# Attention and FFN on one core: sums of W_out kept in SBUF, W_in read back from DRAM for each batch, k and v loaded in two halves, sums formed on VectorE

## The chip, the cores and the metric

One core of one Trainium2 chip runs one program. The metric is the device time of one execution in microseconds (us), lower is better; several executions are timed and their median is compared. The engines are PE (TensorE, with PEld for its weight loads), DVE (VectorE), ACT (ScalarE), POOL (GpSimd) and SP (SyncE, which issues nearly all DMAs of this kernel). A profile is one further execution, recorded by the hardware.

## The reference

```python
a = softmax(phi, over the 32 memory slots)                 # 8 batches, 8 heads, 576 rows
k_m = einsum('bhsm,bhsd->bhmd', a, k); v_m = einsum('bhsm,bhsd->bhmd', a, v)
attn = softmax(q @ k_m.T / 8)                              # 576 x 32 per head
x = (attn @ v_m) as rows of 512                            # 4608 x 512
h = x @ w_in;  g = h * sigmoid(h);  out = g @ w_out        # 512 -> 2048 -> 512
```

All is float32. The sums `k_m` and `v_m` are first divided by their softmax sums.

## The kernel before, in words

**Numbers in two parts.** A float32 operand is cut into a high and a low part in a format that TensorE multiplies in one pass (F32R). A product is high x high, high x low and low x high. W_out lies in SBUF as `wo_hi` and `wo_lo`, 16 chunks of 128 rows by 512 columns.

**P.** `attn @ v_m @ w_in` is done as `attn @ P` with P = `v_m @ w_in`, which has 256 rows (8 heads x 32) and 2048 columns. `p_mm` (L609) makes a quarter of P (512 columns) from `win` into the PSUM tile `bg`; `p_split` (L626) writes the high part on ACT (L629) and the low part on DVE (L631). W_in lies in the SBUF tile `win` all the time. P's homes are `pparts` (two quarters) and, from batch 2 on, two tiles `pm` for the other two.

**Batches 0 and 1** run 16 steps, one per chunk of 128 hidden columns: `ffn1` (h), `silu`, `split`, then `main_step` against the chunk of W_out into four PSUM banks. Batch 0 also converts the weights. The rows beyond 512 of two batches are handled together after each odd batch (`left_split`, `left_step`, later `left_st`).

**Batches 2 to 7** use the seven products of Strassen and Winograd instead of eight, on blocks of two row tiles by two chunks by two halves of columns. A batch has two halves `t` of eight steps `j`; one step is, in PE's order, `ffn1s` (12 matmuls into the PSUM tile `h`, L783), then what the table of events puts in that step, then `st_step` of the step before (21 matmuls, L814, into four banks `sum`). `forms` makes the seven left operands from silu: ACT writes `gbuf` (L794) and the first three high parts (L798), DVE the sums in `gbuf` (L799, L802, L803), the other four high parts (L804) and all the low parts `gparts` (L805). The silu of the next step writes the same `gbuf`, so it waits for L805. After the eighth step `st_out` combines the four banks: ACT copies two (L846), DVE does seven operations of 128x256 (L851), and SP stores the result (L862).

The seven right operands are four plain blocks of W_out (one of them replaced by the sum T1, `t1_load`) and three more sums of blocks. The sums are made once, in batch 1, by `w_forms`: POOL adds (L747 to L752), ACT and DVE cut the result into high and low parts in a tile `ring` (L755, L756), and a DMA writes it to DRAM (`saved`). From batch 2 on, each step reads three of them back into the four places of `ring`: `ring_load` asks for the next one after each use, 288 loads of 256 KB in all. In `st_step` the held blocks come first (8 matmuls with high left parts, 4 with low ones), then the three from the ring with 3 matmuls each. The four banks are filled in the order 0, 1, 2, 3.

**The order of the work.** PE's and (from batch 1) ACT's instructions stand as the code records them; DVE's and SP's are ordered by the scheduler. The attention for batch n = b + 1 is spread over the steps of batch b by a table of slots, `at_slot` (L921 to L925): `mx, sub, ex, em, tr, s0, s1, sx, se, ss, sn, sk` are the steps of the phi maximum, its fold and subtraction, its exp, `e_mm` (k_m and v_m from phi and the four k/v chunks), the transposes, the scores, their maximum, exp, sum, norm, and the way back. `p_mm` for the next batch is at steps 10, 12 and 14, its last quarter at step 0 of that batch. `load_kv` fetches the four k/v chunks (516 KB each) and a rest of the next batch right behind `e_mm`. The scores `s_all` use spare columns of the PSUM tile `h`, so the next `ffn1s` waits until DVE has turned them (L376, L378).

Of the kernel before, what the change touches and what calls it, by code (L numbers as in the profile page):

```python
# [19 lines left out]
P = 128  # L20
# [28 lines left out]
def attn_ffn_kernel(  # L49
# [19 lines left out]
    win = const.tile([P, NFC, NR, P], F32, name="win")  # L69
# [6 lines left out]
    pparts = const.tile([P, 2, 2, 2 * JW], F32R, name="pparts")  # L76
# [44 lines left out]
    raws, cvas, last_silu, last_split = {}, {}, [], []  # L121

    def w_load(w, part=None, few=False):
# [3 lines left out]
        if w not in raws:  # L127
            if w in HOMES:
                home = win[:, HOMES[w] : HOMES[w] + 4].rearrange("p k r f -> p (k r f)")
                raws[w] = home.bitcast(I64).rearrange("p (k f) -> p k f", k=2)  # L130
            else:
                raws[w] = sb.tile([P, 2, DMODEL], I64, tag="raw", name="raw", bufs=RAWB)
# [15 lines left out]
    def w_conv(w, part=None, steps="pcsahl"):  # L148
# [7 lines left out]
        if kind == "i":  # L156
            to = win[:, fc].rearrange("p k r f -> p k (r f)")
# [65 lines left out]
    def load_kv(b):  # L223
        queue = nc.scalar if b == 0 else None
        ts = []
        for c in range(FULLC):
            t = sb.tile([P, 2, NR, KVW], F32, tag="kv", name=f"kv{b}_{c}", bufs=FULLC)
            load(t.rearrange("p g r f -> p (g r f)"), kv[b, :, c * KVC : (c + 1) * KVC], queue=queue)
            ts.append(t)
        t = sb.tile([P, NR, KVW], F32, tag="kr", name=f"kr{b}", bufs=1)  # L230
        load(t.rearrange("p r f -> p (r f)"), kv[b, :, FULLC * KVC :], queue=queue)
        at[b]["kv"], at[b]["kr"] = ts, t
# [83 lines left out]
    def e_mm(b):  # L316
        e, er, kvt, kr = (at[b][k] for k in ("e", "er", "kv", "kr"))
        pt = beside_h(KVW) if b == 2 else banks(b)
        turns = [(c, p) for c in range(FULLC) for p in range(2)]
        if b == 0:  # L320
            turns.sort(key=lambda t: t[1])
        for c, p in turns:
            for r in range(NR):
# [5 lines left out]
                )  # L329
        for r in range(NR):  # L330
# [161 lines left out]
    def f_copy(u):  # L492
        if u == 0:
            first["left"] = sb.tile([P, P], F32, tag="mx", name="sleft", bufs=1)
        t = first["main", u] = sb.tile([P, 2, 2 * P], F32, tag="kv", name=f"sT{u}", bufs=FULLC)
# [98 lines left out]
    pj, more = {}, []  # L594

    def p_home(b, j):
        if b > 1 and j < 2:
            if not more:
                more.extend(sb.tile([P, 2, 2 * JW], F32R, tag="raw", name=f"pm{k}", bufs=RAWB) for k in range(2))
            home = [more[k][:, j] for k in range(2)]  # L600
        else:
            home = [pparts[:, k, j % 2] for k in range(2)]
        pj[b, j] = [x.rearrange("p (g f) -> p g f", g=2) for x in home]

    def p_mm(b, f, w, low=True):
        j = f // JW
        if f % JW == 0:
            p_home(b, j)
        hi, lo = pj[b, j]  # L609
        c = slice(f % JW, f % JW + w)  # L610
        bg = bgtile()
        kvT = at[b]["kvT"]
        for r in range(NR):
            for p in range(2):
# [3 lines left out]
                    win[D * p : D * (p + 1), f // P : (f + w) // P, r],  # L618
                    start=True, stop=True, skip_group_check=True,
                )  # L620
        if low:
# [73 lines left out]
    def store(key, rows, last=False):  # L695
        if key[0] == 0:
            o = sb.tile([P, DMODEL], F32, tag="raw", name="o", bufs=RAWB)
# [30 lines left out]
    saved = [hbm.tile([P, 4, DMODEL], F32, name=f"forms{j}") for j in range(NP)]  # L728
    ring = []
# [8 lines left out]

    def w_forms(j, step):


        if not ring:
            ring.append(sb.tile([P, 4, DMODEL], F32R, tag="raw", name="ring", bufs=RAWB))
        if step == 0:
            f = at[0]["forms", j] = sb.tile([P, 2, DMODEL], F32, tag="cva", name="wf", bufs=1)
            c = slice(2 * j, 2 * j + 2)
            nc.gpsimd.tensor_tensor(f, as_f32(wo_hi[:, c]), as_f32(wo_lo[:, c]), op=ALU.add)  # L747
            b11, b12, b21, b22 = (f[:, k, q * Q : (q + 1) * Q] for k in range(2) for q in range(2))
            nc.gpsimd.tensor_tensor(b11, b12, b11, op=ALU.subtract)
            nc.gpsimd.tensor_tensor(b12, b22, b12, op=ALU.add)  # L750
            nc.gpsimd.tensor_tensor(b22, b22, b11, op=ALU.add)
            nc.gpsimd.tensor_tensor(b21, b22, b21, op=ALU.subtract)  # L752
# [3 lines left out]
        nc.vector.tensor_tensor(ring[0][:, :, Q:], f, ring[0][:, :, :Q], op=ALU.subtract)  # L756
# [447 lines left out]
```

## Time and profile before

| | |
|---|---|
| median of 3 runs | 743.29 us (742.35 to 745.4) |
| the profiled execution | 746.09 us, of which the span from first to last instruction is 744.3 us |
| PE, PEld busy | 695.1, 602.6 us |
| DVE, ACT, POOL busy | 547.5, 305.8, 50.6 us |
| DMA | 146.36 MB, mean 197 GB/s |
| ring loads | 288 of 256 KB, 3.9 us from issue to landing in the median |

The profiled execution is 2.8 us above the median, 0.4%. Batch 0 ends near 106 us, batch 1 with its left rows near 212 us, batch 2 near 294.6, batch 3 near 391.6, batch 4 near 473.6, batch 5 near 572.5, batch 6 near 651.4 us.

How to read it: an engine's busy time is an average over stages. A row of the waits says which engine and line waited for whom, the sum in us, how often, and the longest. A row of the chain of waits is a piece of the sequence that ended last. A row of the groups has the operation with its tiles, out before in, its shape, the count, busy us and mean ns of one, and the idle time in front of it. "PEld" rows are weight loads, one ahead of each matmul.

### The profile page before, as it was taken

Reading aid. Unit: us, or ns where it says so; the run is one execution under the profiler, and the core shown is the slowest. Engines: PE = TensorE matmul, PEld = TensorE weight load, DVE = VectorE, ACT = ScalarE, POOL = GpSimd, SP = SyncE. Lnnn points to the kernel's source line nnn. Section 1 sums busy time; section 2 is a strip of 40 time slices with the busy share of each in tenths; the row PEclk is TensorE's granted clock in tenths of the full one; section 3 lists DMA queues with packets and bytes.
Section 4 is the critical chain, followed back from the end, with each engine's and each line's share of the span. In section 5 each row is a group of like instructions: output and inputs, shape, how many; then the busy total and the mean of one; then the engine's idle time right before and its main releaser. Section 6 shows DMA issues by size and latency. Waiting matters only on the chain.

```text
span 744.3 us, 15025 instructions
## 1 busy us (share of the span) xinstructions
PE 695.1 (93%) x5932; PEld 602.6 (81%) x5932; DVE 547.5 (74%) x1056; ACT 305.8 (41%) x565; POOL 50.6 (7%) x46
## 2 busy tenths in 40 slices
PE   8999989889899899888999899899899999999996
PEld 3577768777788788887899888788788989889896
DVE  4997897567876689748887579966678669766663
ACT  4877854423525243433424334442431525332320
POOL 0000030667300000000000000000000000000000
PEclk9999999999999999999999999999999999999999
DMA  9996721634566876587653876579564555566661
GB/s 343 309 329 202 290 90 72 230 126 177 209 188 190 294 210 186 159 263 249 191 171 99 259 242 201 148 198 311 163 188 131 144 157 179 164 192 178 194 187 54
DMA packets 70390, 146.36 MB, mean 197 GB/s; under 512 B 7088, under 2 KB 17456, under 8 KB 69296
## 3 DMA queue, kind: packets, MB, share of 16 engines
q1 hardware_dynamic: 69376, 142.63, 60.7%
q10 hardware_dynamic: 944, 2.77, 0.9%
q8 instruction: 47, 0.77, 0.4%
q14 instruction: 23, 0.19, 0.1%
HBM read 127.55 MB, written 17.83 MB: 195 GB/s over the span
## 4 chain that ended last, share of the span: by engine, by line
PE 47%; DMA 17%; DVE 14%; POOL 3%; ACT 3%; issue 3%; SPq 0%; DVEq 0%; ACTq 0%
PE sum L814 20%; DMA ring<-forms 17%; PE h L783 12%; PE lsum L814 5%; PE acc L691 3%; PE bg L615 2%; PE h L650 2%; DVE gparts L805 2%; PE accleft L691 1%; POOL wf L747 1%; DVE oo L851 1%; PE bg L324 1%; DVE pm L631 1%; DVE ring L756 1%; ACT gbuf L794 1%
## 5 line engine op out<-in xcount | busy, mean ns | idle before, releaser
L794 ACT ACTIVATE gbuf<-h 128x512 f32<-128x512 f32 x96 | 57.5, 599 | 297.5 <-PE h L783 209.1
L814 PE MATMUL sum<-ring,aparts 128*128 128x256 f32 x576 | 116.3, 293 | 22.2 <-DMA ring<-forms 18.2
L814 PEld LDWEIGHTS sum<-ring,aparts 128*128 128x128 f32 x576 | 88.1, 190 | 35.0 <-DMA ring<-forms 28.6
L805 DVE TENSOR_TENSOR gparts<-gbuf,aparts 128x896 fp32r<-128x896 f32 x96 | 104.5, 1088 | 9.0
L799 DVE TENSOR_TENSOR gbuf<-gbuf 128x256 f32<-128x256 f32 x96 | 40.8, 425 | 87.1 <-ACT gbuf L794 86.9
L814 PE MATMUL sum<-wo_hi,aparts 128*128 128x256 f32 x384 | 98.8, 290 | 0.0
L814 PE MATMUL sum<-wo_lo,aparts 128*128 128x256 f32 x384 | 95.5, 282 | 0.0
L783 PE MATMUL h<-aparts,pm 128*128 128x288 f32 x576 | 85.6, 298 | 5.4 <-DVE sc L378 5.4
L691 PE MATMUL acc<-wo_hi,gparts 128*128 128x512 f32 x256 | 87.6, 402 | 2.4 <-DVE gparts L667 2.2
L814 PEld LDWEIGHTS sum<-wo_hi,aparts 128*128 128x128 f32 x384 | 72.5, 189 | 17.4 <-issue 11.1
L783 PEld LDWEIGHTS h<-aparts,pm 128*128 128x128 f32 x576 | 79.6, 191 | 6.4 <-issue 6.3
L783 PE MATMUL h<-aparts,pparts 128*128 128x288 f32 x576 | 83.8, 294 | 0.0
L814 PE MATMUL sum<-ring,gparts 128*128 128x256 f32 x288 | 80.6, 280 | 0.0
L783 PEld LDWEIGHTS h<-aparts,pparts 128*128 128x128 f32 x576 | 78.1, 188 | 0.0
L814 PEld LDWEIGHTS sum<-wo_lo,aparts 128*128 128x128 f32 x384 | 72.7, 189 | 0.0
L814 PE MATMUL sum<-wo_hi,gparts 128*128 128x256 f32 x384 | 63.0, 286 | 1.3 <-DVE gparts L805 0.8
L650 PEld LDWEIGHTS h<-aparts,pparts 128*128 128x128 f32 x372 | 52.7, 192 | 13.0 <-issue 2.9
L650 PE MATMUL h<-aparts,pparts 128*128 128x288 f32 x372 | 57.4, 304 | 6.0 <-ACT gleft L677 2.2
L691 PEld LDWEIGHTS acc<-wo_hi,gparts 128*128 128x128 f32 x256 | 48.5, 191 | 17.2 <-DVE gparts L667 4.9
L814 PEld LDWEIGHTS sum<-wo_hi,gparts 128*128 128x128 f32 x384 | 52.6, 191 | 3.5 <-DVE gparts L805 3.1
L814 PEld LDWEIGHTS sum<-ring,gparts 128*128 128x128 f32 x288 | 54.2, 188 | 0.0
L691 PE MATMUL acc<-wo_lo,gparts 128*128 128x512 f32 x128 | 51.1, 399 | 1.0 <-DVE wo_lo L178 0.9
(199 smaller groups left out, 1055.3 us busy)
## 6 DMA issues: line engine op xcount, KB each, us to landing
ring<-forms SPq DMA_DIRECT2D x288, 256.0 KB, 3.9
kv<-in_kv SPq DMA_DIRECT2D x28, 516.0 KB, 6.9
q<-in_q SPq DMA_DIRECT2D x16, 576.0 KB, 6.2
forms<-ring SPq DMA_DIRECT2D x8, 1024.0 KB, 4.1
raw<-in_w_in SPq DMA_DIRECT2D x14, 512.0 KB, 6.3
out<-oo SPq DMA_DIRECT2D x27, 256.0 KB, 2.4
raw<-in_w_out SPq DMA_DIRECT2D x6, 1024.0 KB, 5.0
phi<-in_phi SPq DMA_DIRECT2D x7, 576.0 KB, 4.9
```

The source lines that it names most:

```text
L324: nc.tensor.matmul(pt[p][M * r : M * (r + 1), :KVW], e[:, p, c, M * r : M * (r + 1)], kvt[c][:, p, r], start=c == 0, stop=False, skip_grou ...
L615: nc.tensor.matmul(bg[M * r : M * (r + 1), p, :w].rearrange("p (k f) -> p k f", f=P), kvT[D * p : D * (p + 1), 1, r], win[D * p : D * (p + ...
L631: nc.vector.tensor_tensor(lo[:, :, c], bg[:, :, :w], hi[:, :, c], op=ALU.subtract)
L650: nc.tensor.matmul(h[:, hf, :HALF], wt[:, p, fs], a[:, p, hf * HALF : (hf + 1) * HALF], start=n[hf] == 0, stop=n[hf] == 5, skip_group_chec ...
L691: nc.tensor.matmul(acc[key], gt[:, cs], wt[:, fc], start=fc == 0 and n == 0, stop=fc == NFC - 1 and n == 2)
L747: nc.gpsimd.tensor_tensor(f, as_f32(wo_hi[:, c]), as_f32(wo_lo[:, c]), op=ALU.add)
L756: nc.vector.tensor_tensor(ring[0][:, :, Q:], f, ring[0][:, :, :Q], op=ALU.subtract)
L783: nc.tensor.matmul(h[:, i, :HALF], wt[:, p, f : f + P], a[:, p], start=n == 0, stop=n == 5)
L794: nc.scalar.activation(gbuf[:, :MAIN].rearrange("p (i f) -> p i f", i=2), h[:, :, :w], AF.Silu)
L799: nc.vector.tensor_tensor(g[:, 4:6], g[:, :1].broadcast_to([P, 2, P]), g[:, 1:3], op=ALU.subtract)
L805: nc.vector.tensor_tensor(lo, g[:, 1:], hi, op=ALU.subtract)
L814: nc.tensor.matmul(sums[bank][:, place * Q : (place + 1) * Q], gt[:, k], wt, start=bank not in begun, stop=True, skip_group_check=True,)
```

## The change

- The three sums per step stay in SBUF as `kept`, 24 tiles of 128x512 float32 (high and low halves side by side); `ring`, `ring_load` and the 288 loads are gone. Only T1 still goes through DRAM.
- The room comes from W_in and from two k/v chunks. W_in is in four tiles `w0` to `w3`; in batch 0 `win_save` writes them to DRAM, and in batch 1 `kept` takes their places. From batch 2 on, `win_load` brings a quarter of W_in (1 MB) into the very place `h0` to `h3` in which that quarter of P will lie, `p_mm` reads it from there, and then the parts of P overwrite it. A quarter can come when the last `ffn1s` of the batch that reads the old P is done.
- From batch 3 on `load_kv` and `e_mm` go in two halves: chunks 0 and 1 are used at step 5, chunks 2 and 3 come into the same two places and are used at step 7.
- `w_forms` adds on DVE instead of POOL.
- `st_step` does all seven high parts first, then all seven low ones, and fills the banks in the order 0, 3, 1, 2.
- The slots move: the tables below the code show it.

```diff
     def w_forms(j, step):
...
         if step == 0:
+            while len(kept) < 3 * j + 3:
+                keep(*homes_left.pop(0))
             f = at[0]["forms", j] = sb.tile([P, 2, DMODEL], F32, tag="cva", name="wf", bufs=1)
             c = slice(2 * j, 2 * j + 2)
-            nc.gpsimd.tensor_tensor(f, as_f32(wo_hi[:, c]), as_f32(wo_lo[:, c]), op=ALU.add)
+            nc.vector.tensor_tensor(f, as_f32(wo_hi[:, c]), as_f32(wo_lo[:, c]), op=ALU.add)
...
-        nc.scalar.activation(ring[0][:, :, :Q], f, AF.Copy)
-        nc.vector.tensor_tensor(ring[0][:, :, Q:], f, ring[0][:, :, :Q], op=ALU.subtract)
-        load(saved[j], as_f32(ring[0]))
...
+        for t, i, e in runs:
+            src, to = f[:, n : n + e - i], t[:, i:e]
+            nc.scalar.activation(to[:, :, :Q], src, AF.Copy)
+            nc.vector.tensor_tensor(to[:, :, Q:], src, to[:, :, :Q], op=ALU.subtract)
+            n += e - i
+        load(saved[j], as_f32(t1[:, 0]))
...
-        held = ((0, 0, 0, b11), (0, 1, 2, b21), (1, 0, 6, b22), (1, 1, 4, b12))
+        t3, t4, t2 = ((x[:, :Q], x[:, Q:]) for x in kept[3 * j : 3 * j + 3])
+        todo = (
+            (0, 0, 0, b11), (0, 1, 2, b21), (3, 0, 1, t4), (1, 0, 6, b22), (1, 1, 4, b12), (2, 0, 5, t2), (2, 1, 3, t3)
+        )
         for terms in (HIGH, LOW):
-            for bank, place, k, w in held:
+            for bank, place, k, w in todo:
                 product(bank, place, part, k, w, terms)
-        for bank, place, k in ((2, 0, 5), (2, 1, 3), (3, 0, 1)):
-            r = ring[0][:, next(used) % 4]
-            product(bank, place, part, k, (r[:, :Q], r[:, Q:]), HIGH + LOW)
-            ring_load()
...
+    win_saved = [hbm.tile([P, 4, NR, P], F32, name=f"win_saved{k}") for k in range(4)]
+
+    def win_save():
+        for k in range(4):
+            load(win_saved[k], win[k])
+
+    def win_load(b, k):
+        t = wins[b, k] = sb.tile([P, 4, NR, P], F32, tag=f"h{k}", name=f"win{b}_{k}", bufs=1)
+        load(t, win_saved[k])
...
-                ev(b, 1.5 * j + 3, w_forms, j, 1)
+                ev(b, 1.5 * j + 2.5, w_forms, j, 1)
         else:
-            ev(b, 0, p_mm, b, (3 if b > 2 else 2) * JW, JW)
-            if b == 2:
-                ev(b, 2, p_mm, b, 3 * JW, JW)
-            else:
+            ev(b, 0, win_load, b, 3)
+            ev(b, 1, p_mm, b, 2 * JW, JW)
+            ev(b, 3, p_mm, b, 3 * JW, JW)
+            if b > 2:
...
-            else (0, 1, 3, 5, 6, 7, 7, 9, 10, 11, 11, 13)
+            else (1, 2, 4, 5, 8, 9, 9, 10, 11, 12, 13, 14)
...
+            ev(b, em, e_mm, n, range(2))
+            ev(b, em, load_kv, n, range(2, FULLC))
+            ev(b, em + 2, e_mm, n, range(2, FULLC))
+            if n + 1 < B:
+                ev(b, em + 2, load_kv, n + 1, range(2))
...
-            for j in range(3):
-                ev(b, 10 + 2 * j, p_mm, n, j * JW, JW)
+            for k in range(3):
+                ev(b, 6 + k if b == 1 and k < 2 else 10 + 2 * k, win_load, n, k)
+            for k in range(2):
+                ev(b, (12 if b == 1 else 13) + 2 * k, p_mm, n, k * JW, JW)
```

DVE's order in the middle of batch 2, around the turning of the scores into `sc`, before (steps 7 and 8; `x<-sum` is the first operation of `st_out`):

```order
L376 STREAM_TRANSPOSE sc_2434<-bg 128x512
L805 TENSOR_TENSOR gparts<-gbuf,aparts 128x896
L376 STREAM_TRANSPOSE sc_2434<-bg 128x512
L378 STREAM_TRANSPOSE sc_2434<-h 128x64 x2
L413 TENSOR_REDUCE smx<-sc_2434 128x36
L417 TENSOR_TENSOR sc_2434<-sc_2434,smx 128x1152
L799 TENSOR_TENSOR gbuf<-gbuf 128x256
L802 TENSOR_TENSOR gbuf<-gbuf 128x128
L803 TENSOR_TENSOR gbuf<-gbuf 128x128
L804 CAST aparts<-gbuf 128x512
L851 TENSOR_TENSOR x<-sum_2083,oo 128x256
L805 TENSOR_TENSOR gparts<-gbuf,aparts 128x896
```

The same place after (steps 8 and 9; lines have moved by some twenty, so L874 is `st_out`, L823 to L829 is `forms`, L387 and L389 turn the scores):

```order
L874 TENSOR_TENSOR oo<-oo 128x256
L874 TENSOR_TENSOR oo<-x,oo 128x256
L874 TENSOR_TENSOR oo<-x,sum_2121 128x256
L823 TENSOR_TENSOR gbuf<-gbuf 128x256
L826 TENSOR_TENSOR gbuf<-gbuf 128x128
L387 STREAM_TRANSPOSE sc_2573<-bg 128x512
L827 TENSOR_TENSOR gbuf<-gbuf 128x128
L387 STREAM_TRANSPOSE sc_2573<-bg 128x512
L828 CAST aparts<-gbuf 128x512
L389 STREAM_TRANSPOSE sc_2573<-h 128x64
L829 TENSOR_TENSOR gparts<-gbuf,aparts 128x896
L389 STREAM_TRANSPOSE sc_2573<-h 128x64
```

The turning of the scores stood a step ahead of `st_out`; now all seven operations of `st_out` are ahead of it, and the last turn out of `h` stands behind the low parts.

DVE's order where batch 2 ends and batch 3 begins, before (`pparts<-bg` is the low part of the last quarter of P, `aparts<-aT` the low part of the attention's second half):

```order
L631 TENSOR_TENSOR pparts<-bg,pparts 128x1024
L851 TENSOR_TENSOR x<-sum_2574,oo 128x256
L851 TENSOR_TENSOR x<-sum_2574,x 128x256
L851 TENSOR_TENSOR oo<-oo 128x256
L851 TENSOR_TENSOR oo<-x,oo 128x256
L851 TENSOR_TENSOR oo<-oo 128x256
L851 TENSOR_TENSOR oo<-x,oo 128x256
L851 TENSOR_TENSOR oo<-x,sum_2575 128x256
L799 TENSOR_TENSOR gbuf<-gbuf 128x256
L802 TENSOR_TENSOR gbuf<-gbuf 128x128
L452 TENSOR_TENSOR aparts<-aT_2784,aparts 128x2x288
L803 TENSOR_TENSOR gbuf<-gbuf 128x128
```

And after (`mt` is the start of the next phi maximum, `pm` the low part of the third quarter of P):

```order
L823 TENSOR_TENSOR gbuf<-gbuf 128x256
L874 TENSOR_TENSOR oo<-oo 128x256
L874 TENSOR_TENSOR oo<-x,oo 128x256
L874 TENSOR_TENSOR oo<-x,sum_2608 128x256
L826 TENSOR_TENSOR gbuf<-gbuf 128x128
L256 TENSOR_TENSOR mt<-phi_2849 128x512
L827 TENSOR_TENSOR gbuf<-gbuf 128x128
L646 TENSOR_TENSOR pm<-bg,pm 128x1024
L828 CAST aparts<-gbuf 128x512
L463 TENSOR_TENSOR aparts<-aT_2844,aparts 128x2x288
L829 TENSOR_TENSOR gparts<-gbuf,aparts 128x896
L257 TENSOR_TENSOR mx<-mt 128x256
```

The low part of P moved from ahead of `st_out` to behind it, into the middle of `forms` of step 0, and the phi maximum joined it there.

DVE's order early in batch 1, before (L665 and L667 are the split of the ordinary step; `wf` is the sum of blocks that POOL has formed, five rows per group on POOL):

```order
L667 TENSOR_TENSOR gparts<-gbuf,gparts 128x512
L756 TENSOR_TENSOR ring<-wf,ring 128x4x256
L665 CAST gparts<-gbuf 128x512
L667 TENSOR_TENSOR gparts<-gbuf,gparts 128x512
L756 TENSOR_TENSOR ring<-wf,ring 128x4x256
```

And after (L680 and L682 are the split; `t` and `kept` are the low parts of the sums):

```order
L769 TENSOR_TENSOR wf<-wo_hi,wo_lo 128x1024
L771 TENSOR_TENSOR wf<-wf 128x256
L772 TENSOR_TENSOR wf<-wf 128x256
L680 CAST gparts<-gbuf 128x512
L773 TENSOR_TENSOR wf<-wf 128x256
L682 TENSOR_TENSOR gparts<-gbuf,gparts 128x512
L774 TENSOR_TENSOR wf<-wf 128x256
L680 CAST gparts<-gbuf 128x512
L789 TENSOR_TENSOR t_1370<-wf,t_1370 128x256
L682 TENSOR_TENSOR gparts<-gbuf,gparts 128x512
L789 TENSOR_TENSOR kept<-wf,kept 128x256
L789 TENSOR_TENSOR kept<-wf,kept 128x2x256
```

Five additions and two or three subtractions per group now stand between the casts of the ordinary steps.

More of the change, by code (lines that the diff above doesn't have):

```diff
@@ L727, in attn_ffn_kernel @@
     TF = 7 * P
[L728 to L729 removed]
+    saved = [hbm.tile([P, DMODEL], F32, name=f"forms{j}") for j in range(NP)]
+    kept, kept_at = [], []
+    homes_left = [("r2", 4), ("w0", 4), ("w1", 4), ("kv2", 2), ("kv3", 2), ("w2", 4), ("w3", 4)]
     form_src = gbuf.rearrange("p (n f) -> p n f", f=P)
```

111 lines of the change are left out of this document (58 added, 53 removed).

## The prediction

> **What bounds the kernel now.** I read the page first, then the busy time by batch, then the waits, then the chain of waits. The page says how full the engines are and what the end hung on:
>
> ```profile
> PE 695.1 (93%) x5932; PEld 602.6 (81%) x5932; DVE 547.5 (74%) x1056; ACT 305.8 (41%) x565; POOL 50.6 (7%) x46
> ...
> PE 47%; DMA 17%; DVE 14%; POOL 3%; ACT 3%; issue 3%; SPq 0%; DVEq 0%; ACTq 0%
> ```
>
> TensorE is full most of the time, yet 17% of the chain runs through DMA and 14% through DVE. By stretches (time, then busy us of PE, PEld, DVE, ACT and POOL, granted clock, DMA share, GB/s): batch 1 without its left rows, batch 3, batch 6 and batch 7.
>
> ```profile
> 106.00:200.00 94.00, 84.87 (x599) 68.15 (x600) 66.70 (x92) 37.34 (x61) 44.08 (x36) 0.96 0.40 151
> 294.60:391.60 97.00, 89.64 (x818) 81.31 (x817) 74.01 (x156) 34.44 (x68) 0.00 (x0) 1.00 0.68 206
> 572.50:651.40 78.90, 76.69 (x728) 69.94 (x727) 60.19 (x118) 32.82 (x65) 0.00 (x0) 1.00 0.52 152
> 651.40:744.30 92.90, 84.76 (x663) 80.49 (x661) 54.21 (x114) 23.70 (x57) 0.00 (x0) 0.99 0.55 161
> ```
>
> Batch 1 wastes 9.1 us of PE, batch 3 7.4 us, batch 6, in which no k and v are loaded any more beside the ring, only 2.2 us. Who PE waited for (sum in us, times, longest):
>
> ```profile
> PEld sum L814 <- DMA ring<-forms: 28.6, 51, 2.4
> ...
> PEld sum L814 <- DVE oo L851: 4.0, 8, 1.2
> ...
> PE h L783 <- DVE sc L378: 5.4, 5, 1.1
> ...
> PEld sum L814 <- DVE gparts L805: 3.1, 9, 0.7
> ```
>
> ```profile
> ACT gbuf L794 <- DVE gparts L805: 77.9, 23, 5.3
> ```
>
> The ring is the largest wait, 51 times. The last row is the second bound: the silu of a step waits for DVE's low parts of the step before, since both use `gbuf`. What a step costs with no wait, from the chain (start, us, what):
>
> ```profile
> 410.93 1.58 PE h L783 x12
> 412.51 2.48 PE sum L814 x21
> ```
>
> So 4.06 us a step: 0.118 us a product.
>
> **The change, part by part.**
>
> *The ring goes.* A weight load takes 190 ns (the group row below) but one starts every 118, so each idle row is short by 0.07 us: 28.6 + 51 x 0.07 = 32.2 us. I take this; 28.6 is the low end, and 46.8 the high one, if PE's own 18.2 us never overlapped with them.
>
> ```profile
> L814 PE MATMUL sum<-ring,aparts 128*128 128x256 f32 x576 | 116.3, 293 | 22.2 <-DMA ring<-forms 18.2 <-DVE oo L851 2.0 <-DVE x L851 0.7
> ...
> L814 PEld LDWEIGHTS sum<-ring,aparts 128*128 128x128 f32 x576 | 88.1, 190 | 35.0 <-DMA ring<-forms 28.6 <-DVE oo L851 4.0 <-DVE x L851 1.1
> ```
>
> Nothing is late next by DMA alone: the 24 W_in quarters are 24 MB for the ring's 72. Each quarter is asked for three steps before its `p_mm`, at least 12 us, and a load of that size took 8.1 us at worst; two k/v chunks have from step 5 to step 7, 8.1 us plus half of `e_mm`, against 6.9 for all five loads of a batch. I set both at 0; the cover is those steps. The saves in batch 0 lie beside the conversions: 0.
>
> ```profile
> kv<-in_kv SPq DMA_DIRECT2D x28, 516.0 KB, 6.9
> ...
> win<-in_w_out SPq DMA_DIRECT2D x1, 1024.0 KB, 8.1
> ```
>
> SP's queue loses 288 issues that waited for PE. A `win_load` now waits there for the last `ffn1s` on its quarter, with q loads and a store behind it that nobody needs for several steps: 0.
>
> *Low parts last.* The 7 low products start after 14 products instead of 8, 0.7 us later, which is the longest of those nine waits: -3.1 us.
>
> *Scores behind st_out.* Means of the operations (ns behind the busy us):
>
> ```profile
> L805 DVE TENSOR_TENSOR gparts<-gbuf,aparts 128x896 fp32r<-128x896 f32 x96 | 104.5, 1088 | 9.0
> ...
> L804 DVE CAST aparts<-gbuf 128x512 fp32r<-128x512 f32 x96 | 41.0, 427 | 9.0 <-DVE gbuf L803 0.9
> L799 DVE TENSOR_TENSOR gbuf<-gbuf 128x256 f32<-128x256 f32 x96 | 40.8, 425 | 87.1 <-ACT gbuf L794 86.9
> ...
> L803 DVE TENSOR_TENSOR gbuf<-gbuf 128x128 f32<-128x128 f32 x96 | 27.8, 290 | 3.0
> L802 DVE TENSOR_TENSOR gbuf<-gbuf 128x128 f32<-128x128 f32 x96 | 27.7, 289 | 2.8
> ...
> L851 DVE TENSOR_TENSOR oo<-oo 128x256 f32<-128x256 f32 x24 | 10.0, 418 | 0.1
> ...
> L376 DVE STREAM_TRANSPOSE sc<-bg 128x512 f32<-128x512 f32 x12 | 8.4, 704 | 0.0
> ...
> L378 DVE STREAM_TRANSPOSE sc<-h 128x64 f32<-128x64 f32 x12 | 2.0, 207 | 0.0
> ```
>
> `forms` is 2.5 us of DVE, the four turns 1.8. Before, they began 0.65 us (ACT's silu) after `ffn1s` and ended at 4.95; PE had s_all and 2.48 of products, and waited 5.4/5 = 1.1, so s_all is 4.95 - 1.1 - 2.48 = 1.4 us. After, counted from the last product of step 7, DVE does 7 x 0.42 + 2.5 + 1.8 = 7.3 us and is done at 7.95; PE has 1.58 + 1.4 + 2.48 = 5.45 and waits 2.5. That is 1.4 more, in batches 2 to 6: +7 us. Bank 3, now the third to be filled, is read last by `st_out` (3.6 us after the last product); with s_all in between the wait is 0.2 and lies inside the 2.5, in batch 7, without s_all, it is 1.5: +1.5.
>
> *The seam of two batches.* In batches 3, 5 and 7, DVE does `st_out` (2.9), the first sum of `forms` (0.4), two short ones (0.6), `mt` and the low part of P before the cast:
>
> ```profile
> L631 DVE TENSOR_TENSOR pm<-bg,pm 128x1024 fp32r<-128x1024 f32 x12 | 14.6, 1217 | 0.0
> ...
> L249 DVE TENSOR_TENSOR mt<-phi 128x512 f32<-128x512 f32 x7 | 4.8, 687 | 1.3 <-ACT oo L705 1.1 <-DMA phi<-in_phi 0.2
> ```
>
> With the cast 0.43 that is 6.3 us after the last product. PE gets there after `ffn1s` 1.58, `p_mm` about 1.2 and six products on ACT's parts 0.7: it waits 2.8, then about 0.9 for the low parts, 0.5 more in the next step. Together 4.2. The weight-load row above has 4.0 + 1.1 us of waits for the banks of `st_out`; an estimate of a third of that per seam, 1.7, is there already, so +2.5 net, three times, +7.5. Batches 4 and 6 follow the left rows, which cover most of it: +1 each, +2.
>
> *Sums on DVE, in batch 1.* The trace has no such sum on DVE; a two-input operation of 1024 columns is 1.22 us (`pm`), of 256 columns 0.42, so 8 x (1.22 + 4 x 0.42) = 23 us more DVE. What falls away: DVE operations that overlap POOL's are stretched (the first is POOL's, the second DVE's in the same moment):
>
> ```profile
> 158.34 2.50 POOL L747 TENSOR_TENSOR wf<-wo_hi,wo_lo 128x1024 f32<-128x1024 f32 x1 [2.44 <-DVE ring L756]
> ```
>
> ```profile
> 158.71 2.69 DVE L667 TENSOR_TENSOR gparts<-gbuf,gparts 128x512 fp32r<-128x512 f32 x1
> ```
>
> ```profile
> L667 DVE TENSOR_TENSOR gparts<-gbuf,gparts 128x512 fp32r<-128x512 f32 x32 | 28.5, 891 | 1.5
> ...
> L665 DVE CAST gparts<-gbuf 128x512 fp32r<-128x512 f32 x32 | 18.8, 587 | 18.0 <-ACT gbuf L675 18.0
> ...
> L667 DVE TENSOR_TENSOR gparts<-gleft,gparts 128x512 fp32r<-128x512 f32 x9 | 6.2, 687 | 0.2
> ...
> L665 DVE CAST gparts<-gleft 128x512 fp32r<-128x512 f32 x9 | 3.8, 422 | 2.7 <-PE accleft L691 1.5 <-PE acc L691 1.2
> ```
>
> The same operations on the left rows, when POOL is silent, take 687 and 422: 32 x (0.204 + 0.165) = 11.8 us of stretch go. DVE ends 11 us fuller, 78 of the 94 us of the stretch above. It fits, but barely, since DVE's and ACT's queues wait for each other there (ACT's copy of a sum stands ahead of the next silu, as it stood before behind POOL). Of what PE lost,
>
> ```profile
> PE h L650 <- ACT gleft L677: 2.2, 1, 2.2
> PE acc L691 <- DVE gparts L667: 2.2, 1, 2.2
> PE h L650 <- ACT kvT L356: 2.1, 1, 2.1
> PE h L324 <- ACT gleft L677: 1.4, 1, 1.4
> ```
>
> the four largest are 7.9 us, while POOL works for 44 of the 94 us; in the last of the four in time, in a row below, it works for 2.24 of 2.40. The bounds are -12 (9.1 us of PE's idle time and two stretches of half clock, below, gone) and +11 (all of DVE's new work on the path); I take -6, since the row that is nearest, the stretch, is shown to go, and the load that comes is spread over twelve steps.
>
> *The sum.* -32.2 - 3.1 + 7 + 1.5 + 7.5 + 2 - 6 = -23.3 us. The profiled execution took 746.1 us, of which 744.3 are span; the median of the runs is 743.3, so I forecast 746.1 - 23.3 = 722.8 for such an execution and **720.0 us** for the median.
>
> **The rivals.**
>
> *The seams cost nothing.* If the scheduler's order lets `st_out` start earlier (bank 0 and 1 are copied before the last products) and the 14 high products hide the cast, the 18 us of new waits shrink to 3, and it comes to 705 us. For it: DVE still has slack, 87.1 us of idle time in front of the 96 L799. Against it: the chain of waits already ran through these operations for whole steps. 0.18.
>
> *DVE becomes the bound of batch 1.* There DVE is 71% busy (66.7 of 94) and waits for silu in between; if it idles as long as before, 27 us, with 78 us of work, the stretch takes 105 instead of 94: +11 instead of -6, 737 us. For it: DVE and ACT run in order and wait for each other every step. Against it: much of that idle time was waiting for POOL's sums by way of ACT. 0.17.
>
> *The clock halves at each seam.* After PE has stood still, the granted clock is 0.50 for 3.4 us:
>
> ```profile
> 187.10:189.50 2.40, 0.41 (x2) 0.00 (x0) 2.40 (x3) 2.37 (x4) 2.24 (x3) 1.00 0.72 290
> 189.50:192.90 3.40, 3.15 (x12) 2.90 (x12) 3.33 (x5) 0.85 (x3) 2.56 (x3) 0.50 0.02 7
> ```
>
> In the first stretch PE worked for 0.41 of 2.4 us; then twelve matmuls took 3.2 us instead of 1.58, 1.6 more. My waits of 2.5 and 2.8 us are of that length. If all ten halve the clock, that is +16: 736 us. Against it: the clock of batch 1 is 0.96 on the mean, which over 94 us is two such stretches, for four long waits. 0.10. The Trainium skill ("TensorE: Matmul & The Clock Gate", "Why this matters for your kernels") puts the limit at idle gaps of about 3 us. By that rule no seam halves the clock, and the sum stays; the trace does not agree, since here a gap of 2.4 us was enough.
>
> *Slower: W_in comes late.* Each of the 24 `p_mm` reads a quarter that must have left SP's queue, landed, and must be multiplied before P's parts can replace it. The point from which it decides is a landing of 12 us after the last `ffn1s` that frees the place. Were each load held that long and 1.5 us more by what stands ahead of it on SP, 24 x 1.5 = 36 us would be added: 756 us, slower. For it: SP is in order and `out` and phi wait there for DVE. Against it: 8.1 us was the worst landing of such a size, with DMA far busier. 0.05.
>
> *The waits are only renamed.* If most ring rows hid a wait for DVE that lasted as long, as the row of bank waits (4.0) does for eight places, the ring would bring 12 us instead of 32, and the new seams take it: 740 us, no change that can be told. For it: the chain through L805. Against it: batch 6, with the same DVE work and an unhurried ring, wastes only 2.2 us of PE. 0.04.
>
> **How the numbers follow.** My forecast has 0.44; the rest, 0.02, is for what I have not seen, on the slow side. The first rival (705) and the upper ones (736, 737) must be mostly inside, so the range is 703 to 738; what it leaves out is half the tails of these, late W_in and renamed waits, some 0.2. A measurement of this kernel can tell about 0.5%, 3.7 us, from no change. Faster by more than that, under 739.6: the forecast, the first rival, most of the second and third, 0.85. Within 0.5%: the upper tails of the second and third and the last rival, 0.09. Slower: W_in late and a part of what I have not seen, 0.06.
>
> **What the profile after would show.** No row with `ring`; DMA down by some 50 MB (75 of the ring less 25 of W_in); the PE rows with `kept` wait for DVE (`oo`, `gparts`), not for DMA. "PE h <- DVE sc" grows from 5.4 to some 12 us in five waits. The first step of batches 3, 5 and 7 has a wait of 2 to 3 us in front of `kept` or `wo_hi` products. POOL is empty, the casts of batch 1 are all at 0.42 us, and the stretch of batch 1 is some 6 us shorter. I am wrong if PE waits for `win` or `kv` from DMA, if batch 1 grows, or if batch 6, which had little of the ring's waits, is shorter than 75 us or longer than 82.

## The result, and the profile after

The changed kernel takes 712.06 us in the median of 4 runs (710.69 to 712.24), the kernel before 743.09 us (742.35 to 745.4; the 743.29 above is the median of three of these four runs): a ratio of 0.9573, with a 95% interval of 0.9549 to 0.9597. The forecast was 720.0 us in a range of 703 to 738. The profiled execution took 712.11 us with a span of 710.2, where the forecast for such an execution was 722.8: the sum of its terms was -23.3 us, and the two profiles differ by 34.1 us in span. (By the medians it is 31.0: the profiled execution of before lay 3 us above its median.)

Lines of the first, third and fourth parts of the page, after:

```profile
PE 682.6 (96%) x5932; PEld 601.2 (85%) x5932; DVE 549.4 (77%) x1109; ACT 307.6 (43%) x578; POOL 0.7 (0%) x6
...
DMA packets 32946, 93.88 MB, mean 132 GB/s; under 512 B 2928, under 2 KB 13296, under 8 KB 29296
...
PE 55%; DVE 22%; ACT 5%; issue 3%; DVEq 0%; ACTq 0%
```

DMA has left the chain of waits (17% before), and DVE has taken a part of its place (14% before, 22% now). By stretches, with the columns of the prediction: batch 1 with its left rows, batches 2 and 3, batches 6 and 7.

```profile
106.00:200.90 94.90, 93.33 (x653) 75.96 (x654) 80.75 (x166) 40.46 (x77) 0.00 (x0) 1.00 0.41 142
200.90:280.10 79.20, 77.10 (x714) 70.59 (x713) 57.03 (x113) 32.49 (x64) 0.00 (x0) 0.98 0.36 124
280.10:370.80 90.70, 87.30 (x817) 80.64 (x816) 73.39 (x156) 34.59 (x68) 0.00 (x0) 1.00 0.32 113
...
541.50:621.00 79.50, 77.28 (x728) 71.22 (x726) 61.12 (x131) 32.78 (x65) 0.00 (x0) 0.98 0.23 74
621.00:710.20 89.20, 82.98 (x679) 80.16 (x677) 57.05 (x117) 24.64 (x58) 0.00 (x0) 0.99 0.07 25
```

Batch 1 with its left rows, 106 us before (106.0 to 212.0), is 11.1 us shorter; batch 3 went from 97.0 to 90.7 us; batch 6, which had little of the ring's waits, from 78.9 to 79.5. The clock shows 0.98 in batches 2, 4 and 6, and otherwise 1.00 but for the very end. Who PE and its weight loads waited for:

```profile
PE h L807 <- DVE sc L389: 10.0, 5, 2.0
PE bg L333 <- ACT phi L317: 1.7, 2, 1.0
...
PE sum L838 <- DVE oo L874: 1.3, 1, 1.3
```

```profile
PEld sum L838 <- DVE oo L874: 2.3, 4, 1.5
...
PEld sum L838 <- DVE gparts L829: 1.5, 5, 0.3
```

No row of DMA is left. The five waits for the scores grew from 5.4 to 10.0 us, and a new one stands in front of `e_mm` (L333).

To put sizes on all of this, I took from both traces each matmul's start, the time to the next start, and what this is above the median of its kind in that run. Only what is late by more than 0.1 us is counted. The sums for batches 2 to 7, in us, by the matmul that started late:

```
                                         before   after
products on ring / kept, high parts        38.0     2.5
products with low parts                     4.0     2.3
h of the next step                          7.3    12.3
first matmuls of e_mm                       0.5     3.6
p_mm                                        8.8     8.8
held blocks, high parts (*)                14.4    18.0
left rows; the rest                         6.2     6.8
all                                        79.2    54.3
(*) most of it first products behind p_mm, e_mm, s_all
```

### The profile page after: what moved, and what is told of

It reads as the page before. It is cut to its first block, busy times and chain, and to the rows that moved or that the text cites. A ratio compares the mean times of both kernels' runs of the same rounds, so it can differ in the third digit from the quotient of the medians.

```text
span 710.2 us, 14595 instructions
## 1 busy us (share of the span) xinstructions
PE 682.6 (96%) x5932; PEld 601.2 (85%) x5932; DVE 549.4 (77%) x1109; ACT 307.6 (43%) x578; POOL 0.7 (0%) x6
## 4 chain that ended last, share of the span: by engine, by line
PE 55%; DVE 22%; ACT 5%; issue 3%; DVEq 0%; ACTq 0%
PE sum L838 20%; PE h L807 15%; PE acc L706 6%; PE lsum L838 5%; DVE gparts L829 4%; PE h L665 4%; PE bg L628 2%; DVE oo L874 2%; DVE pm L646 2%; ACT gbuf L818 2%; DVE gbuf L823 2%; PE accleft L706 2%; PE bg L333 1%; DVE aparts L828 1%; DVE aT L453 1%
## 5 line engine op out<-in xcount | busy, mean ns | idle before, releaser
L807 PE MATMUL h<-aparts,pm 128*128 128x288 f32 x1152 | 170.9, 298 | 10.0 <-DVE sc L389 10.0
L807 PEld LDWEIGHTS h<-aparts,pm 128*128 128x128 f32 x1152 | 158.7, 190 | 11.0 <-issue 10.8
L829 DVE TENSOR_TENSOR gparts<-gbuf,aparts 128x896 fp32r<-128x896 f32 x96 | 104.7, 1091 | 8.4
L838 PE MATMUL sum<-wo_hi,aparts 128*128 128x256 f32 x384 | 105.6, 297 | 0.0
L838 PE MATMUL sum<-kept,aparts 128*128 128x256 f32 x576 | 101.2, 284 | 1.5 <-DVE oo L874 1.3
L823 DVE TENSOR_TENSOR gbuf<-gbuf 128x256 f32<-128x256 f32 x96 | 40.7, 424 | 78.3 <-ACT gbuf L818 78.0
L838 PEld LDWEIGHTS sum<-wo_hi,aparts 128*128 128x128 f32 x384 | 74.2, 193 | 20.9 <-issue 12.7
L838 PEld LDWEIGHTS sum<-kept,aparts 128*128 128x128 f32 x576 | 83.5, 193 | 2.3 <-DVE oo L874 2.3
L838 PE MATMUL sum<-wo_hi,gparts 128*128 128x256 f32 x384 | 73.8, 284 | 0.5
L838 PE MATMUL sum<-kept,gparts 128*128 128x256 f32 x288 | 65.5, 282 | 0.0
L665 PEld LDWEIGHTS h<-aparts,pm 128*128 128x128 f32 x372 | 51.7, 188 | 8.6 <-issue 2.3
L665 PE MATMUL h<-aparts,pm 128*128 128x288 f32 x372 | 56.3, 299 | 1.9 <-DVE aparts L463 1.0
L822 ACT ACTIVATE aparts<-gbuf 128x384 fp32r<-128x384 f32 x96 | 50.4, 525 | 0.0
L838 PEld LDWEIGHTS sum<-kept,gparts 128*128 128x128 f32 x288 | 47.9, 190 | 0.0
L828 DVE CAST aparts<-gbuf 128x512 fp32r<-128x512 f32 x96 | 40.7, 424 | 8.1 <-DVE phi L313 0.3
```

The source lines that it names most:

```text
L665: nc.tensor.matmul(h[:, hf, :HALF], wt[:, p, fs], a[:, p, hf * HALF : (hf + 1) * HALF], start=n[hf] == 0, stop=n[hf] == 5, skip_group_chec ...
L807: nc.tensor.matmul(h[:, i, :HALF], wt[:, p, f : f + P], a[:, p], start=n == 0, stop=n == 5)
L822: nc.scalar.activation(hi[:, :3], g[:, 1:4], AF.Copy)
L823: nc.vector.tensor_tensor(g[:, 4:6], g[:, :1].broadcast_to([P, 2, P]), g[:, 1:3], op=ALU.subtract)
L828: nc.vector.tensor_copy(hi[:, 3:], g[:, 4:])
L829: nc.vector.tensor_tensor(lo, g[:, 1:], hi, op=ALU.subtract)
```

## The experiments

The kernel before scatters by some 1% from run to run and chip to chip (738.0 to 747.6 us over all its runs); the executions of a changed version lie within 0.6% of each other. Variants of the changed kernel are therefore compared by their own medians and by the rows of their traces, and ratios are to the kernel before on the same chip. Runs 1 to 4, 5 to 8, 9 and 10, and 11 and 12 had one chip each. An undisturbed step (step 6 of batch 3) takes 4.10 or 4.11 us in the traces of the changed kernel and of runs 4 to 9, 11 and 12, so medians from these chips can be set side by side; the ratios, which carry the scatter of the kernel before, give the differences told below the same signs but other sizes (run 6: 2.5 us below the changed kernel, run 7: 11.5 above, run 9: 5.4 below).

**1 to 4: the two halves of the gain.** In the kernel before, the ring loaded once (1), the sums on DVE (2), both (3); in the changed kernel, the sums on POOL again (4).

```diff
 # 1
-        if u is not None:
+        if u is not None and u < 4:
             j, k = uses[u]
 # 2 (five operations of w_forms); 4 is the reverse
-            nc.gpsimd.tensor_tensor(f, as_f32(wo_hi[:, c]), as_f32(wo_lo[:, c]), op=ALU.add)
+            nc.vector.tensor_tensor(f, as_f32(wo_hi[:, c]), as_f32(wo_lo[:, c]), op=ALU.add)
```

> The kernel before, in which the four places of the ring are loaded once and never again: 284 of the 288 loads are left out, so the products use old sums. Theory (the ring's landings held PE up): the starts in front of ring products are late by 38.0 us in all, of which about 6 wait for the banks of st_out, so 32 us go and it comes to 711 us (705 to 716). Rival (the waits are only renamed, DVE's low parts and banks take their place): about -12 us, 731 us.

Measured: 717.72 us, ratio 0.9664 (0.9648 to 0.9680), 24.7 us by the medians and 28.0 us between the profiles. The waits of the weight loads, where the kernel before had 28.6 for the ring, 4.0 for the banks and 3.1 for the low parts:

```profile
PEld sum L814 <- DVE gparts L805: 6.8, 15, 0.7
...
PEld sum L814 <- DVE oo L851: 4.5, 9, 1.2
```

The ring was the wait, and an eighth of it came back: by the starts, products on the ring are late by 6.9 us instead of 38.0, and those with low parts by 7.7 instead of 4.0. The truth lies between theory and rival, near the theory.

> The kernel before with the sums of blocks added on DVE instead of POOL, nothing else. Theory (POOL's additions stretched DVE's operations and kept ACT waiting): batch 1 gets shorter by 9 to 11 us, 733 us, and the casts of batch 1 are at 0.42 us. Rival (the gain of the first 200 us came from the new places and slots): within 2 us of the kernel before. Third (DVE becomes the bound of batch 1): 754 us.

Measured: 730.96 us, ratio 0.9841 (0.9820 to 0.9861). Batch 2 begins at 201.0 us instead of 212.0:

```profile
106.00:201.00 95.00, 93.46 (x653) 75.43 (x652) 79.19 (x147) 39.24 (x63) 0.00 (x0) 1.00 0.50 183
```

This one edit carries the whole gain of the first two batches: DVE is busy 79 of 95 us, and PE idles for 1.5. The rivals (the new slots; DVE as the bound) fall.

> Both edits together on the kernel before: no reloads (284 loads left out) and the sums on DVE. If the two causes are apart, their gains add, -32 and -10: 701 us. The change itself stands at 712 us, so what keeping the sums costs in other places (W_in from DRAM, k and v in halves, later slots) would be 11 us. Rival (the first batches and the ring overlap): 710 us or more.

Measured: 706.91 us, ratio 0.9519 (0.9503 to 0.9535), 35.5 us, against 24.7 + 11.5 = 36.2 for the two alone: they add. The change itself has 31.0 of that, so all that it does to make room for the sums costs 4.5 us, net of what its new order of products gains.

> The changed kernel with only the additions of w_forms back on POOL. Theory: batch 1 grows by 9 to 13 us, 723 us, the casts of batch 1 rise from 0.42 us to some 0.59 us, and PE waits for gleft and gparts there. Rival (the first 200 us got shorter by the slots and places): 712 to 715 us.

Measured: 716.17 us, 4.1 us above the changed kernel, with a batch 2 that begins at 206.1 us, 5.2 later. This is less than half of what was expected, though the stretch of DVE's operations is back in full: the casts of batches 0 and 1 take 593 ns in the mean of all 32, as expected, against 418 in the changed kernel. Two of the four long waits are there:

```profile
PE acc L706 <- DVE gparts L682: 2.2, 1, 2.2
PE h L365 <- ACT gleft L692: 1.7, 1, 1.7
```

but no stretch of half clock follows one here, and before there were two in batch 1 (at 107.6 and 189.5 us, 1.6 us each). So the 11 us are what POOL's sums cost at the old slots; what the half slot by which `w_forms` moved, or the smaller pieces that it writes, took off that was not tried apart.

**5: the order of products.** In the changed kernel the order of before:

```diff
-        for terms in (HIGH, LOW):
-            for bank, place, k, w in todo:
-                product(bank, place, part, k, w, terms)
+        held = ((0, 0, 0, b11), (0, 1, 2, b21), (1, 0, 6, b22), (1, 1, 4, b12))
+        for terms in (HIGH, LOW):
+            for bank, place, k, w in held:
+                product(bank, place, part, k, w, terms)
+        for bank, place, k, w in ((2, 0, 5, t2), (2, 1, 3, t3), (3, 0, 1, t4)):
+            product(bank, place, part, k, w, HIGH + LOW)
```

> The changed kernel with the order of products of before: held blocks with high parts, held blocks with low parts, then the three kept sums with three products each, banks 0, 1, 2, 3. Theory of the forecast: the low products start six products earlier, so DVE's low parts are late again, +3.1 us, and bank 3 is last again, -1.5 us in batch 7: 713.5 us. Rival (the low parts were late for other reasons): 710.5 us.

Measured: 713.36 us (712.18 to 713.49; ratio 0.9615, 0.9586 to 0.9644), 1.3 us above the changed kernel. The intervals of the two ratios overlap, so this is near the limit of what can be told; but execution by execution at the same mean clock the difference is there (713.3 to 713.5 us at 0.991 to 0.993 against 712.0 to 712.2 at 0.991 or 0.992, and 712.2 against 710.7 at 0.994). The row is as forecast,

```profile
PEld sum L838 <- DVE gparts L829: 7.2, 15, 0.7
```

1.5 us in 5 waits with the new order. By the starts the low parts cost 5.7 us more, the kept sums 1.9 us less (bank 3 in batch 7 no longer waits) and `e_mm` 1.6 us less. The new order is worth a microsecond or so; what it saves is partly paid elsewhere.

**6 and 9: the scores.** In step 9 of batches 2 to 6 the DVE part of `forms` behind the turns (6); then also the maximum of the scores behind that `forms` (9).

```diff
-            part = forms(b, t, j, h)
+            part = forms(b, t, j, h)
+            late = s == 9 and b + 1 < B
+            if not late:
+                forms_dve(j)
...
+            if late:
+                forms_dve(j, at[b + 1]["turned"])
 # 9
+        if b > 2:
+            behind(i.ins, last_form[0])
```

> The changed kernel with one order on DVE: in step 9 of batches 2 to 6 the five DVE operations of forms stand behind the four turns of the scores. Theory: the five waits in front of h (2.15 us each by starts) go, and with them the three stretches of half clock behind them (1.5 us each), while the cast of step 9 is up to 0.5 us late for the next products: -10.7 - 4.5 + 2.5 = -12.7, 699 us (696 to 704). Rival (the wait moves on to forms and silu, which share gbuf): 708 to 712 us.

Measured: 707.35 us (707.13 to 708.07), 4.7 us below the changed kernel and not 12.7, just under the rival's 708 to 712. The waits for the scores are gone and so are all halvings of the clock but the one at the very end; but DVE now does this in steps 9 and 10 of batch 2 (start, us, operation):

```profile
248.62 0.34 DVE L389 STREAM_TRANSPOSE sc<-h 128x64 f32<-128x64 f32 x2
248.88 0.39 DVE L828 TENSOR_TENSOR gbuf<-gbuf 128x256 f32<-128x256 f32 x1
249.19 1.34 DVE L424 TENSOR_REDUCE smx<-sc 128x36 f32<-128x1152 f32 x1
250.45 0.28 DVE L831 TENSOR_TENSOR gbuf<-gbuf 128x128 f32<-128x128 f32 x1
250.65 1.35 DVE L428 TENSOR_TENSOR sc<-sc,smx 128x1152 f32<-128x1152 f32 x1
251.91 0.29 DVE L832 TENSOR_TENSOR gbuf<-gbuf 128x128 f32<-128x128 f32 x1
252.24 0.43 DVE L833 CAST aparts<-gbuf 128x512 fp32r<-128x512 f32 x1
```

The scheduler put the maximum and the subtraction, ready a little earlier than before, between the sums of `forms`, and PE waits for the cast:

```profile
PE sum L844 <- DVE aparts L833: 5.1, 5, 1.0
```

> The changed kernel with the turns of the scores ahead of forms of step 9, as in the run with that edit alone, and the maximum of the scores behind the low parts of that forms. Theory: the 1.43 us a batch that stayed there (PE waited for the cast, behind the maximum of 1.34 us and the subtraction of 1.35 us that the scheduler had put between the sums) go as well, 5 x 1.43 = 7.1 us below the run with the turns alone (707.4 us): 700 us. Rival (DVE has too much to do in steps 8 to 10, and the wait moves on to silu of step 11 or 12, which stands on ACT behind the exp of the scores): 705 us or more.

Measured: 704.79 us (703.8 to 705.53; ratio 0.9501, 0.9458 to 0.9543), 7.3 us below the changed kernel, 2.6 below run 6. The wait for the cast is gone; in its place, in front of h of step 13,

```profile
PE h L810 <- ACT gleft L823: 4.8, 5, 1.0
```

since silu of step 12 stands on ACT behind the exp of the scores and waits for the low parts of step 11. In batch 4 the maximum and the subtraction (1.34 and 1.36 us) stand on DVE ahead of `forms` of step 11, and its low parts are done at 427.27 us, 1.5 us after that exp. The theory held for the wait that it named, the rival for where it went. No version tried here is faster than this one.

**7, 8, 10, 11, 12: other slots.** Each edit is in the table or next to it; 8 is 6 and 7 together, 10 and 11 stand on 9, 12 on 11. In 10 the order of 9 on DVE holds for step 10 instead of 9, as the scores do.

```diff
-            else (1, 2, 4, 5, 8, 9, 9, 10, 11, 12, 13, 14)
+            else (0, 1, 3, 5, 8, 9, 9, 10, 11, 12, 13, 14)     # 7, 8
+            else (1, 2, 4, 6, 9, 10, 10, 11, 12, 13, 13, 14)   # 10
+            else (1, 2, 4, 5, 8, 9, 9, 10, 12, 13, 13, 14)     # 11, 12
-        ev(b, 3 if b > 1 else sub + 0.5, phi_sub, n)
+        ev(b, sub + 0.5, phi_sub, n)                           # 7, 8, 12
```

> The changed kernel with the phi maximum, fold, subtraction and exp each one slot earlier, as before the change (slots 0, 1, 1.5, 3). Theory: e_mm no longer waits for the exp and its table load (0.8 and 1.2 us in batches 3 and 5, 0.3 in 4 and 6): -2.6 us, 709.5 us. Rival (DVE has the phi maximum at the seam of two batches, and PE waits there instead): 712 us or more.

Measured: 720.87 us (720.52 to 723.43), 8.8 us slower. `e_mm` is no longer late (1.1 us by the starts instead of 3.6), but the phi maximum and the subtraction now stand on DVE ahead of `st_out` where batch 3 begins, and PE waits for `st_out`:

```profile
284.95 0.50 PE L838 MATMUL sum<-wo_hi,gparts 128*128 128x256 f32 x2 [0.30 <-DVE gparts L829]
290.84 0.38 PE L838 MATMUL sum<-wo_hi,aparts 128*128 128x256 f32 x1 [1.27 <-DVE x L874]
293.22 0.76 PE L838 MATMUL sum<-kept,aparts 128*128 128x256 f32 x4 [1.64 <-DVE oo L874]
```

Batches 3 and 5 take 6 us more each: 5.2 and 5.1 us of this fall into their first three steps, with a stretch of half clock in each. The rival came true, far above its lower bound.

> The changed kernel with the scores turned ahead of forms and the exp one slot earlier. If the two gains are apart: -12.7 - 2.6, 697 us. If both live on the same slack of DVE: 700 us or more.

Measured: 716.73 us (713.74 to 717.65). 7 costs 8.8, 6 brings 4.7: together +4.7, about their sum of 4.1. The theory had counted on a gain from 7, which run 7 did not show.

> The same with the attention from e_mm on one step later (e_mm at 6 and 8, transposes at 9, scores at 10, the way back still at 14), so that e_mm no longer waits for the exp and st_out lies a step ahead of the turns. Theory: the waits in front of e_mm (0.8 and 1.2 us in batches 3 and 5, 0.3 in 4 and 6) go: 2.6 us below the run with the turns and the maximum, 697.5 us. Rival (the norm and the way back are crowded into steps 13 and 14, and the next batch's first h waits): 702 us or more.

Measured: 708.89 us (708.71 to 709.2), 4.1 us above run 9. The waits in front of `e_mm` are gone, as in 7; PE waits for the banks of `st_out` (5.2 us in 9 waits, 1.2 in run 9), because the scaling of `kvn`, a step later, now stands on DVE just ahead of it, and for the cast of step 13 (4.7 us), with the sum, norm and way back around it as the rival had it.

> The kernel with the turns ahead of forms and the maximum behind it, and the exp of the scores one slot later (12 instead of 11, sum and norm both at 13). Theory: the wait of 1.13 us in front of h behind step 12, which came from silu of step 12 standing on ACT behind that exp, and 0.5 us behind it, go in five batches: 704.8 - 5 x 1.6 = 697 us. Rival (sum, norm, turn back and the low part of P now all stand in steps 13 to 15 on DVE, and the low parts of forms are late there): 703 us or more.

Measured: 709.92 us (709.06 to 710.36), 5.1 us above run 9 (2.4 by the ratios). The wait for h is gone, and the sum, the reciprocal and the norm stand in one piece in front of `forms` of step 13:

```profile
342.82 1.35 DVE L439 TENSOR_REDUCE ssm<-sc 128x36 f32<-128x1152 f32 x1 [0.20 <-ACT sc L435]
...
344.84 1.36 DVE L445 TENSOR_TENSOR sc<-sc,ssm 128x1152 f32<-128x1152 f32 x1
...
349.34 0.38 DVE L836 CAST aparts<-gbuf 128x512 fp32r<-128x512 f32 x1
```

```profile
PE sum L847 <- DVE aparts L836: 9.8, 5, 2.0
```

Behind three of these five waits the clock halves, which run 9 does not have. The rival came true.

> The same with the subtraction of the phi maximum half a slot earlier (2.5 instead of 3), the maximum and the fold where they are. Theory: the exp, and with it e_mm, is ready 1.0 us earlier, which takes most of the 3.1 us of waits in front of e_mm: 2 us below the run before it. Rival (the subtraction and the low part of P now stand ahead of the cast of step 3 on DVE, and PE waits there instead): the same or 1 to 4 us more.

Measured: 712.81 us (711.47 to 713.17), 2.9 us above run 11. The rival came true: PE now waits for the cast of step 3 (0.9 us each in batches 3 and 5), and the wait in front of `e_mm` stayed (4.2 us by the starts, 3.4 in run 11).

## Why the prediction was right, point by point

The sign, the size (712.06 in the range, -4.2% for -3.1%) and the large causes held. The sums below are for the profiled executions; "by the starts" is the table above.

**Ring and low products: -35.3 forecast, -39.7 by the starts** (38.0 + 4.0 before, 2.3 after; the 2.5 on `kept` belong to bank 3 and the seams). The correction of 0.07 us a row was right: 32.2 for the ring, 31.1 fell away in run 1. What I left out is that the waits for banks in the same rows go too. In run 1, without the ring, they are the 6.9 us that stayed, 4.4 of them where batches 3 and 5 begin; after the change they are 2.5. The new order of banks is not the reason, since run 5, with the old one, has only 0.6. Before, the low part of P (1.22 us on DVE) stood ahead of `st_out` there, and the change put it behind; I take this for the cause, but no run tried it alone.

**Scores behind st_out: +7 forecast.** The waits grew from 1.24 to 2.15 us by the starts, five times, +4.6; my 2.5 was close. Behind three of the five, the next step took 5.7 instead of 4.18 us at half clock, +4.5; the kernel before had one such stretch in these batches, behind a wait for the ring in batch 5, with 1.2 us outside the ring's row, so +3.3 net. Together +7.9. The mechanism stands: in batch 2 the last product of step 7 is done at 243.4 us and the last turn at 250.8, 7.4 us for the 7.3 that were worked out. The 0.65 us for silu, which the prediction put ahead of these to come to 7.95, did not show.

**Bank 3 in batch 7: +1.5 forecast, 1.53 measured.**

**The seam of two batches: +7.5 forecast, +1.0 measured. This step failed.** It had DVE with `st_out`, the sums, `mt` and the low part of P in front of "the cast", 6.3 us after the last product, and PE at that cast "after `ffn1s` 1.58, `p_mm` about 1.2 and six products". The time on DVE was right. But the rows of the order that I read are `forms` of step 1, not of step 0 (the section on the change says step 0, too, and is wrong there). DVE's and PE's rows of the changed kernel, from the end of batch 2 (start, us):

```profile
282.51 0.43 DVE L823 TENSOR_TENSOR gbuf<-gbuf 128x256 f32<-128x256 f32 x1
...
283.70 0.43 DVE L828 CAST aparts<-gbuf 128x512 fp32r<-128x512 f32 x1
...
284.19 1.74 PE L807 MATMUL h<-aparts,pm 128*128 128x288 f32 x12
...
285.27 0.42 DVE L874 TENSOR_TENSOR x<-sum,oo 128x256 f32<-128x256 f32 x1
...
286.92 0.42 DVE L823 TENSOR_TENSOR gbuf<-gbuf 128x256 f32<-128x256 f32 x1
```

```profile
289.27 1.22 DVE L646 TENSOR_TENSOR pm<-bg,pm 128x1024 fp32r<-128x1024 f32 x1
...
289.82 1.74 PE L807 MATMUL h<-aparts,pm 128*128 128x288 f32 x12
290.40 0.42 DVE L828 CAST aparts<-gbuf 128x512 fp32r<-128x512 f32 x1
...
291.40 0.28 PE L838 MATMUL sum<-wo_hi,aparts 128*128 128x256 f32 x1
...
292.11 0.28 PE L838 MATMUL sum<-wo_hi,aparts 128*128 128x256 f32 x1
```

The sums and the cast of step 0 (282.5 to 284.1) are done before `st_out` begins. The cast behind `st_out`, from 290.4 to 290.8, is first needed by the product at 292.1: the six from 291.4 on stand on ACT's parts, and all of them behind a `p_mm`, 21 products and two `ffn1s`. PE has 7.9 us and not 3.5, and 1.3 us to spare. What is left is 0.33 us for a bank, three times. The 4.4 us that banks cost at the same place in run 1 are gone; that gain stands in the ring's term. Batches 4 and 6, forecast at +2, show nothing. This is one half of the first rival (0.18), though for another reason than its own, that `st_out` starts early. Run 7 shows how thin the cover is: with the phi maximum there as well, 5 us a seam appear.

**e_mm: forecast 0, about +4.5.** Nothing in my text looked at the exp, which the table moves a slot closer to `e_mm`. Its table load and the exp, 1.28 + 1.16 us, end as `e_mm` should start:

```profile
303.20 1.28 ACT L317 ACT_TABLE_LOAD   x1
304.49 1.16 ACT L317 ACTIVATE phi<-phi 128x1152 f32<-128x1152 f32 x1
305.71 0.82 PEld L333 LDWEIGHTS bg<-kv,phi 128*32 128x32 f32 x32 [0.88 <-ACT phi L317]
```

These waits are 2.6 of the 3.1 us by which the row grew (0.5 to 3.6). The two halves of `e_mm` cost 0.4 us more per batch than the one (5.30 + 5.68 - 4.07 against 6.53 by steps of batch 2), 1.9 in five batches (the other 0.5 us of the row is a part of this): PE's change from one kind of matmul to the other is paid twice. The cover that I named for the k and v loads held, though its 6.9 us were the median of one load and not of all five (before, those of one batch took from 139.8 to 150.7 us): in batch 2 the second two chunks are asked for at 226.4 us, are there at 231.7 and are used at 235.1.

**The first two batches: -6 forecast, -11.1 measured**, at the low end of its bounds (-12 to +11). Run 2 gives -11.5 for this edit alone. The four long waits and both half-clock stretches went; the casts are at 418 ns (32 of them), as worked out, and DVE's 23 us of new sums were all beside PE's work, although DVE is 85% busy there (80.75 of 94.9). The cover that I doubted, DVE's idle time between silu and silu, was enough.

The terms for batches 2 to 7 are then -39.7 + 7.9 + 1.5 + 1.0 + 4.5 = -24.8, and the table has 54.3 - 79.2 = -24.9. The batches themselves went from 532.3 us to 509.3, -23.0; most of the difference lies in the medians, which the table leaves out (a product with a high part takes 0.120 us on `kept` and 0.118 on the ring). With -11.1 for the first two it is -34.1. That the time fell into the range was in part luck: the terms for the ring, the scores' waits, the seams and the first two batches came out 20.4 us better than forecast, and what was forecast at nothing (clock, e_mm, medians) took 9.7 us of this back. Without the latter the time would have been below 703 us. The rival of the half clock (0.10) came true in three of its ten places. W_in was never waited for; its 24 loads landed in 4.7 to 7.3 us.

## What to carry to other kernels

When a transfer is taken out of a full schedule, look for the next thing that is late in each step: here it was DVE, and each of six attempts to move its work (runs 6, 7 and 9 to 12) brought a new wait elsewhere; only 6 and 9 gained on the version that they changed. Before a row of an order is given a cost, find out which step it belongs to and when its reader comes; being one step off was the main error of the seams. And two engines side by side are not two times as fast: while POOL added, DVE's casts of other tiles took 0.59 us in the mean instead of 0.42. What this costs depends on the schedule: PE lost 11 us by POOL's sums in the old slots and 4 in the new ones.

## What the runs showed of the hardware

**When the clock halves.** Five waits of the same length, 2.0 us, stand in batches 2 to 6 of the changed kernel; the clock halved behind three. The rows of PE alone (stretch, us, busy us, clock, DMA share, GB/s), for the wait of batch 2 and for that of batch 3:

```profile
248.17:251.59 3.42, 1.43 (x12) 1.00 1.01 359
251.59:255.00 3.41, 3.41 (x17) 0.50 0.71 291
326.68:330.09 3.41, 2.33 (x20) 1.00 0.91 307
330.09:333.51 3.42, 2.51 (x19) 1.00 1.02 395
```

In the ten profiles that have more than one stretch of half clock, each stretch begins a whole multiple of 3.413 us after the others of its run (50 and 50 here, 24 and 98 in the kernel before). It lasts one such period (in run 8 two, both times). So there is a fixed grid. In its periods PE was busy for 42% in batch 2, and for 68% and 73% in the two that share the wait of batch 3. Over all 14 profiles, 24 periods within PE's work had a busy share up to 45%, and each was followed by half clock; of 9 between 45% and 52%, five were; of those above, only two, which were at half clock themselves (59% and 64%, in run 8). The Trainium skill ("TensorE: Matmul & The Clock Gate", "What's actually happening") has a free-running window of 3413 ns, and the trace agrees with both; the limit that it gives for gaps does not hold here, since 2.0 us of idle time are enough when they fall into one window. The gap in the kernel before that the prediction gives as 2.4 us is one of 2.24 us in the trace; its window, from 186.1 us, was busy for 41%. Each of the three behind the scores cost 1.5 us, and which waits pay it depends on where they fall on the grid. The executions show it too: three of the changed kernel at a mean clock of 0.991 or 0.992 took 712.0 to 712.2 us, and the one at 0.994 took 710.7.
